# The first stage of the last unit by seven half products

## The chip, the cores and the metric

One core of a Trainium2 chip runs the kernel. The metric is the time of one execution on the device in microseconds. TensorE (PE) multiplies matrices; its weight loads have a row of their own (PEld) and run beside the matmuls. VectorE (DVE) and ScalarE (ACT) read the results from PSUM. GpSimd (POOL) reads SBUF only and issues the loads, and SyncE (SP) issues stores and bounces through HBM.

## The reference

Pooled attention, then a mixer, for 8 batches of 576 rows and 512 columns (8 heads of 64):

```python
k_p = k.reshape(B, H, Sp, pool, D).mean(axis=3)      # pool = 8, so 72 keys
v_p = v.reshape(B, H, Sp, pool, D).mean(axis=3)
attn = softmax(scale * q @ k_p.T)                    # 576 x 72 for each head
x = (attn @ v_p)                                     # as 576 x 512
h = np.maximum(x.T @ w_tok1, 0.0) @ w_tok2           # 576 -> 256 -> 576
u = x + h.T
h2 = np.maximum(u @ w_ch1, 0.0) @ w_ch2              # 512 -> 1536 -> 512
out = u + h2
```

All inputs are fp32; the kernel multiplies in bf16 and adds up in fp32.

## The kernel before

The last two products, `u @ w_ch1` and the one with `w_ch2`, are most of the work. They are done in nine units of 512 rows. Units 0 to 7 take the first 512 rows of batches 0 to 7; unit 8 takes the 8 x 64 rows that are left over, gathered in `uT_tails`.

A unit (`unit_fast`) has two stages. The first makes GT, the maximum with zero of `u @ w_ch1`, transposed: twelve tiles of 128 columns of w_ch1 (`l1_tile`), each of four matmuls 512 columns wide into one PSUM bank, and one evacuation by ScalarE. The second stage multiplies GT by w_ch2 in the way of Strassen and Winograd: seven products of half-sized blocks (`product`, 12 matmuls of 256 columns each) in place of eight. Their operands are sums of blocks of GT, `=3`, `=1`, `=2` and `=4` (`g_sums`, each one VectorE addition of 1536 elements into `area`), and sums of blocks of w_ch2, w0 to w3, made once. In the order of TensorE the products of unit 8 are x, y, z, x again, z again, x again, x again; the other units have an eighth, w. VectorE evacuates them and adds the residual (`plus`); `lo` and `hi` are the two halves of 256 rows of a unit.

A unit is a generator that yields after each half tile (steps 0 to 23) and after each four matmuls of the second stage (24 to 44). `unit` puts other work at the yields, as PLAN says by unit and step: `5.kpT` is the step kpT of batch 5. The names are these.

- `lq`, `lk`, `lv`: the load of a batch's q, k or v, issued by GpSimd's queue and cast to bf16; two buffers each.
- `K0 K1 V0 V1`: pooling of k and v by GpSimd, about 4.3 us each; `kpT`: the pooled keys transposed (TensorE, copied by ScalarE).
- `Q0 Q1`: transposes of q by VectorE (line 284); `s0` to `s2`: scores and exponentials; `av0` to `av4`: times v, divided on VectorE.
- `at0 at1`, `u0` to `u4`: the token products; u ends with a VectorE addition (line 416) into u.
- `M0 M2 M4 M MT`: u out to HBM and back, turned; `T0` to `T5`: its transposes by VectorE into uT (`T4` and `T5` into uT_tails).
- `g`: a gate, one element set by VectorE and copied by GpSimd: what follows in GpSimd's queue waits until VectorE has come so far in its own.

Every engine works through its instructions in the order in which the program lists them. There are four single PSUM banks, p1a to p1d: `take` gives out the one longest given back, and `give` returns a bank as soon as its evacuation is in the program, so a matmul waits on the chip if the bank's last reader isn't done. Scores, av and unit 8's two x tiles use a pair of larger buffers (`p`).

## Time and profile before

| | us |
|---|---|
| median of 3 runs (lowest to highest) | 265.48 (265.43 to 265.86) |
| profiled execution | 264.03 |
| its span, first to last instruction | 262.2 |
| unit 8: first matmul | 239.02 |
| unit 8: second stage begins | 249.38 |
| unit 8: last addition ends | 259.20 |

Times in the text are from the start of the span. A row of the timeline has the start, the length, the engine, the line, the operation, what it writes and reads, the shape and how many, and in brackets how long the engine had been idle and what ended that. A row of the windows has the busy time and the number of instructions of each engine in one stretch.

### The profile page before, as it was taken

The numbers are of one execution on the slowest core, as the hardware profiler recorded it, in microseconds if no ns is written. First come the engines' busy times: TensorE is split into PE (matmuls) and PEld (weight loads), VectorE is DVE, ScalarE is ACT, GpSimd is POOL, SyncE is SP. The second block draws the span as 40 slices with busy tenths as digits, with TensorE's granted clock in tenths as the row PEclk, the third lists the DMA queues.
The fourth block names the chain that finished last, engine by engine and source line by source line (L and its number), as shares of the span: only waits on it lengthen the run. The fifth ranks groups of instructions, "written<-read, shape, count | busy, mean of one in ns | idle before, by whom it ended". The sixth has DMA issues, their size and how long they took to land.

```text
span 262.2 us, 5324 instructions
## 1 busy us (share of the span) xinstructions
PE 255.8 (98%) x2121; PEld 160.4 (61%) x2121; DVE 179.7 (69%) x370; ACT 119.2 (45%) x195; POOL 150.0 (57%) x177
## 2 busy tenths in 40 slices
PE   8899999999999999999999999999999999999994
PEld 3775556754658545864487448744774486486483
DVE  4566489998786657993899449964795486175183
ACT  2445754149465554435641584155535502612610
POOL 8576145999989999999939881988000000101000
PEclk9999999999999999999999999999999999999999
DMA  7999999992096839699357840831414054503204
GB/s 150 191 200 205 206 206 208 207 223 77 2 172 101 133 118 201 146 196 261 66 154 125 239 133 2 162 92 41 123 35 127 5 158 113 129 0 88 75 0 160
DMA packets 31704, 34.29 MB, mean 131 GB/s; under 512 B 3136, under 2 KB 23744, under 8 KB 31680
## 3 DMA queue, kind: packets, MB, share of 16 engines
q0 software_dynamic: 17632, 17.64, 42.6%
q1 hardware_dynamic: 13632, 15.93, 20.4%
q10 hardware_dynamic: 416, 0.39, 0.5%
q8 instruction: 16, 0.26, 0.4%
q14 instruction: 8, 0.07, 0.1%
HBM read 38.99 MB, written 12.58 MB: 197 GB/s over the span
## 4 chain that ended last, share of the span: by engine, by line
PE 80%; POOL 8%; DMA 7%; DVE 3%; issue 1%; POOLq 0%
PE p1d L517 9%; PE p1c L517 9%; PE p1a L517 8%; PE p1b L517 7%; PE p1b L583 7%; PE p1c L583 7%; PE p1a L583 6%; DMA qb<-in_q_dram 5%; PE p1d L583 4%; PE p L297 3%; PE p L379 3%; POOL t L174 2%; POOL t L175 2%; DMA kr<-in_k_dram 2%; PE p L583 2%; PE p1d L393 2%
## 5 line engine op out<-in xcount | busy, mean ns | idle before, releaser
L717 POOL COPY flag<-flag 1x1 f32<-1x1 f32 x47 | 12.6, 269 | 94.5 <-DVE flag L716 94.5
L517 PEld LDWEIGHTS <-w_ch 128*128 128x128 bf16 x432 | 39.6, 98 | 43.4 <-issue 1.8
L583 PEld LDWEIGHTS <-area 128*128 128x128 bf16 x432 | 40.9, 98 | 7.4 <-issue 1.2
L306 ACT ACTIVATE ex<-p 72x768 bf16<-72x768 f32 x42 | 31.6, 803 | 15.9 <-PE p L297 15.7
L583 PEld LDWEIGHTS <-GT 128*128 128x128 bf16 x324 | 30.8, 98 | 8.2 <-issue 2.4
L175 POOL TENSOR_TENSOR t<-t 72x512 f32<-72x512 f32 x23 | 31.0, 1346 | 1.8
L521 ACT ACTIVATE GT<-p1d 128x512 bf16<-128x512 f32 x29 | 17.3, 597 | 27.0 <-PE p1d L517 21.4
L517 PE MATMUL p1d<-uT,w_ch 128*128 128x512 bf16 x104 | 28.8, 379 | 0.0
L174 POOL TENSOR_TENSOR t<-kr 72x1024 f32<-72x1024 bf16 x12 | 25.9, 2155 | 0.5
L517 PE MATMUL p1c<-uT,w_ch 128*128 128x512 bf16 x96 | 26.1, 379 | 0.0
L521 ACT ACTIVATE GT<-p1b 128x512 bf16<-128x512 f32 x26 | 15.6, 598 | 23.2 <-PE p1b L517 16.8
L517 PE MATMUL p1a<-uT,w_ch 128*128 128x512 bf16 x92 | 25.3, 379 | 0.0
L517 PE MATMUL p1b<-uT,w_ch 128*128 128x512 bf16 x92 | 24.2, 379 | 0.0
L174 POOL TENSOR_TENSOR t<-vr 72x1024 f32<-72x1024 bf16 x11 | 24.1, 2187 | 0.3
L521 ACT ACTIVATE GT<-p1a 128x512 bf16<-128x512 f32 x26 | 15.5, 596 | 11.8 <-PE p1a L517 9.2
L521 ACT ACTIVATE GT<-p1c 128x512 bf16<-128x512 f32 x27 | 16.1, 598 | 8.7 <-PE p1c L517 8.3
L384 DVE TENSOR_TENSOR x<-p,den 128x512 bf16<-128x512 f32 x28 | 19.4, 692 | 1.0
L557 DVE TENSOR_TENSOR area<-GT 128x1536 bf16<-128x1536 bf16 x9 | 9.8, 1086 | 12.4 <-ACT GT L521 12.4
L545 DVE TENSOR_TENSOR area<-GT 128x1536 bf16<-128x1536 bf16 x9 | 10.6, 1178 | 10.1 <-ACT GT L521 7.7
L379 PEld LDWEIGHTS <-ex 72*128 72x128 bf16 x280 | 13.4, 98 | 5.6 <-DVE flag L716 0.4
L583 PE MATMUL p1c<-area,area 128*128 128x256 bf16 x120 | 15.4, 273 | 0.0
L379 PE MATMUL p<-vp,ex 72*128 72x65 bf16 x280 | 14.6, 194 | 0.0
(188 smaller groups left out, 461.1 us busy)
## 6 DMA issues: line engine op xcount, KB each, us to landing
out_dram<-o SPq DMA_DIRECT2D x32, 256.0 KB, 4.0
qb<-in_q_dram POOLq DMA_DIRECT2D x7, 576.0 KB, 9.3
kr<-in_k_dram POOLq DMA_DIRECT2D x7, 512.0 KB, 7.4
vr<-in_v_dram POOLq DMA_DIRECT2D x7, 512.0 KB, 9.8
w_ch<-in_moe_w_ch_dram POOLq DMA_DIRECT2D x5, 512.0 KB, 15.8
mem<-u SPq DMA_DIRECT2D x10, 256.0 KB, 2.0
...
```

Of the source, the lines that this page charges most:

```text
L174: eng.tensor_tensor(out=t4[:, 0:n], in0=t[:, hs, 0:4], in1=t[:, hs, 4:8], op=ALU.add)
L175: eng.tensor_tensor(out=t4[:, 0:n, 0:2], in0=t4[:, 0:n, 0:2], in1=t4[:, 0:n, 2:4], op=ALU.add)
L297: nc.tensor.matmul(out=pss[l // 2][0:SP, l % 2, o:o + n1 - n0], lhsT=st["kD"][quad, g, db, :], rhs=st["qD"][quad, g, n0:n1, db], start=(db ...
L306: nc.scalar.activation(out=dst, in_=src, func=AF.Exp, scale=scale)
L379: nc.tensor.matmul(out=ps[:, h // 4, (h % 4) * (D + 1):(h % 4 + 1) * (D + 1)], lhsT=st["ex"][:, h * S + n0:h * S + n0 + P], rhs=st["vp"][: ...
L384: nc.vector.tensor_tensor(out=dst.rearrange("p (a h d) -> p a h d", a=2, d=D), in0=view[:, :, :, 0:D], in1=den[rows, :, :, None].broadcast ...
L517: nc.tensor.matmul(out=ps, lhsT=w_ch1[:, kk, m * P:(m + 1) * P], rhs=uT[kk], start=(kk == 0), stop=(kk == 3))
L521: nc.scalar.activation(out=GT[:, m, :], in_=ps, func=AF.Relu)
L545: nc.vector.tensor_tensor(out=out, in0=a, in1=b, op=ALU.subtract)
L557: nc.vector.tensor_tensor(out=S4[:, 0], in0=GT[:, f, hi], in1=GT[:, sec, hi], op=ALU.add)
L583: nc.tensor.matmul(out=ps[i] if split else ps[:, i], lhsT=chunk(u, i, a(m)), rhs=w(m), start=start and m == 0 and (i == 0 or split), stop= ...
L717: nc.gpsimd.tensor_copy(out=flag[:, 1:2], in_=flag[:, 0:1])
```

## The change

In unit 8 the first stage is also done by seven products of half blocks. Unlike in the second stage, a maximum comes after the blocks are added up, so each of the four output blocks must be complete before it enters GT. The columns of w_ch1 are taken in three groups (a, b, c) of two tiles per half; each group has products 1 to 7, each of four matmuls of 256 columns. Products 1, 6, 7 and 4 add up in one bank and 5 and 3 in a `p` buffer, and 2 has a bank to itself. After products 1, 5 and 6 ScalarE copies the partial sum to SBUF in fp32 (`kept`). Products 2, 3 and 7 are evacuated by a VectorE addition of such a copy, followed by a maximum in place on VectorE or ScalarE (`RELU`); product 4 is evacuated by ScalarE as before. `HALVED` is the order, and the first pieces of x and y of the second stage stand in it.

The operands are sums of blocks of w_ch1 (W0 to W3, in units 6 and 7) and of uT_tails (D80 to D83, in unit 7), all on VectorE, into the buffers that held k and v. PLAN is new for all units: most steps move by a few places, the loads and gates among them. HEAD, the start of the kernel, is unchanged.

```diff
 PLAN = [
-    {0: "0.u3 1.Q0 2.lk 1.kpT", 3: "0.u1", 4: "1.s0 g g", 5: "1.Q1", 9: "1.s1 0.u0", 10: "1.vpool1 1.vpool0 g", 11: "1.s2", 12: "=3 0.u2 2.lq", 13: "1.av1", 14: "1.av3", 16: "1.av2", 18: "w0 3.lk", 19: "1.av0 3.lq", 20: "1.av4 w1 g", 23: "1.at1 2.lv", 24: "1.at0 3.lv =1", 25: "=2 =4", 26: "g", 28: "w3", 31: "1.u1 1.u2", 32: "1.t1", 33: "1.t2 w2", 34: "2.K0", 35: "1.u0", 38: "3.Q1 2.K1", 40: "1.u3", 41: "1.t0", 42: "g", 43: "2.Q0 1.t3", 44: "1.u4 2.V0 2.kpT"},
-    {2: "2.s0", 5: "2.Q1", 6: "2.s2", 9: "3.Q0 3.K0", 11: "3.K1", 12: "2.s1", 16: "2.v1", 17: "4.lq 2.av3 g", 18: "2.av2", 19: "2.av4", 22: "2.av1", 23: "2.av0 =1 =3", 24: "=2", 25: "4.lk g", 26: "g =4", 27: "3.kpT 5.lk 2.at0", 28: "g 3.s1 2.at1", 29: "3.V1", 30: "3.s2 2.u2", 32: "2.u3 3.s0", 33: "2.u0", 37: "2.t3", 39: "2.t0", 40: "2.u1 3.V0", 41: "4.Q1 2.t2", 42: "2.t1", 44: "4.lv"},
-    {2: "3.av4", 3: "3.av0 4.K0", 7: "3.av1", 8: "g 4.K1", 10: "3.av2 3.av3", 13: "g 3.at0", 14: "3.at1 g 6.lk", 16: "4.kpT", 17: "=3", 18: "4.Q0 3.u2", 19: "3.u1", 20: "3.u0", 21: "3.M0", 22: "3.u3 4.s2", 23: "3.M2 4.V1 3.u4", 24: "4.V0", 25: "=1", 26: "=2 3.M4", 27: "4.s0 g", 28: "6.lq", 30: "=4 g", 31: "4.s1 5.lv", 34: "3.M g", 35: "4.av2 3.T1", 36: "3.MT", 38: "3.T2", 40: "3.T3 3.T0", 41: "4.av4", 44: "5.lq 3.T5"},
-    {0: "5.K0 5.K1", 1: "4.av1", 4: "g", 6: "6.lv 4.av0", 7: "4.av3 5.Q0", 9: "5.V1 6.Q0", 10: "4.at1 4.at0", 12: "5.kpT", 13: "4.u2", 14: "4.u1", 15: "g", 16: "5.Q1 4.u3", 17: "5.s0", 19: "3.T4 =3", 21: "4.u0", 23: "=1", 25: "5.V0 4.M0", 26: "=2 5.s1", 27: "g", 29: "=4", 30: "5.s2", 31: "g", 33: "5.av2", 35: "5.av0 5.av1 4.M2 4.M", 39: "5.av3", 40: "4.T2 5.av4", 41: "4.T1", 42: "7.lq 4.T3", 43: "5.at0 4.T0", 44: "5.at1"},
...
-    {18: "=3", 23: "=1", 25: "=2", 30: "=4", 43: "g"},
+    {0: "1.Q0 1.kpT 2.lk 0.u1 0.u3", 3: "1.s0 1.Q1 3.lq", 5: "2.lq g", 9: "1.s1", 10: "g 0.u0 1.vpool0 2.lv", 11: "1.vpool1 1.s2 =3 g", 12: "0.u2", 13: "1.av1", 14: "1.av3", 15: "1.av2", 17: "1.av0", 19: "w0 1.av4", 20: "3.lk g", 21: "3.lv", 23: "w1 1.at1 =1", 24: "=2", 26: "=4", 27: "g w3", 28: "1.at0", 30: "1.u2", 31: "1.u1", 33: "1.t2 1.t1", 34: "2.K0 w2", 36: "1.u0", 39: "3.Q1 1.u3", 40: "2.K1", 43: "1.t0 g 2.Q0 1.t3 1.u4", 44: "2.Q1 2.V0 2.kpT"},
+    {2: "2.s0", 6: "2.s2", 9: "3.K0", 10: "3.K1", 12: "3.Q0 2.s1", 13: "2.v1", 17: "2.av3", 18: "2.av2", 19: "2.av4 4.lq", 21: "g", 22: "2.av0", 23: "2.av1 4.lk", 24: "=1", 25: "g =2", 26: "g 5.lk =3", 27: "=4 3.kpT", 28: "g 2.at0 3.s1 2.at1 3.V1", 31: "3.s2 3.V0 2.u0", 32: "2.u3", 33: "2.u1 3.s0", 34: "2.u2", 37: "2.t3", 39: "2.t0", 41: "4.lv 2.t2", 42: "2.t1", 44: "4.Q1"},
+    {2: "3.av4 4.K0", 5: "3.av0", 7: "g 4.K1 3.av2", 9: "3.av1 g", 11: "3.av3", 13: "3.at0", 14: "3.at1 g =3", 16: "4.Q0", 17: "4.kpT 3.u0", 18: "3.u1", 19: "3.u2", 20: "6.lk", 21: "4.V1 3.M0 3.u3", 22: "4.s2 3.M2 3.u4", 24: "4.V0 g", 25: "4.s0 =1", 27: "6.lq 3.M4", 28: "=2", 29: "=4", 30: "g 4.s1 5.lv", 31: "3.M 3.MT", 32: "g 5.lq", 33: "3.T0", 35: "3.T2", 36: "3.T3", 39: "3.T1", 40: "4.av4", 44: "4.av2"},
+    {0: "5.K1 5.K0 4.av1", 4: "3.T5 g", 5: "6.lv", 6: "5.V1 4.av0", 8: "4.av3", 10: "4.at0 5.Q1 5.Q0 4.at1", 12: "g 4.u2", 13: "6.Q0 5.kpT", 15: "4.u1", 16: "4.u3", 17: "3.T4 5.s0", 18: "=3", 21: "4.u0", 22: "5.V0", 23: "5.s1", 25: "=1", 26: "g", 27: "=2", 29: "5.s2 g", 31: "=4", 32: "5.av1", 33: "4.M0 4.M2 5.av2", 36: "5.av3", 38: "7.lq", 39: "5.av0", 40: "4.M 5.av4 4.T3", 41: "4.T2", 42: "4.T0 4.T1", 43: "5.at0", 44: "6.Q1 5.at1"},
...
+    {5: "6.av0", 6: "6.av1", 7: "7.K0", 8: "6.av3 7.K1", 9: "7.kpT", 12: "6.at0", 13: "7.V0", 14: "7.s1 6.at1", 15: "g 7.V1", 17: "6.u0 6.u3", 18: "6.u2", 20: "6.u1", 21: "6.M2 g", 23: "=3 6.M0", 24: "7.s0 =1", 26: "6.M =2", 27: "=4", 30: "g", 31: "7.av1", 32: "6.T0", 37: "6.T1", 38: "6.T2", 39: "7.s2", 40: "6.T3", 41: "g", 44: "7.av2"},
+    {0: "7.av0", 1: "g", 6: "g", 10: "7.av3", 11: "7.av4", 13: "W0 7.at0", 15: "g 7.at1", 16: "W1", 18: "7.u0", 19: "7.u1", 20: "7.u2 g 7.u3", 21: "=3", 22: "7.M0 g", 24: "g =1 =2", 26: "7.M2", 29: "7.M", 30: "g", 32: "=4", 34: "7.u4 g", 35: "7.T0 7.T1", 36: "7.T2", 37: "7.T3", 38: "7.M4", 41: "g W2", 44: "7.MT g 7.T5"},
+    {1: "g W3", 18: "=3", 20: "g", 22: "g", 23: "=1", 24: "=2", 25: "7.T4", 27: "=4", 32: "D80", 33: "g", 34: "D81", 41: "g", 42: "D82", 44: "D83"},
+    {19: "=3", 21: "=1 =2", 24: "=4", 41: "g"},
...
+    HALVED = {B: "a1 a2 a5 b1 b2 a6 a3 b6 c1 b5 a7 b7 c5 c2 c6 b3 a4 c3 c7 b4 x0 c4 x1 x2 y0 y1 y2"}
+    RELU = dict(a2="D", a3="D", a7="A", b2="D", b3="D", b7="A", c2="D", c3="A", c7="D")
...
+    wide = {}
+
+    def first_weight(k):
+        if k == 0:
+            for key in "kv":
+                t = raw.tile([P, H, POOL, D], BF16, name=key + "r").rearrange("p h i d -> p (h i d)")
+                wide[key] = t[:, 0:4 * DC // 2].rearrange("p (s c n) -> p s c n", s=2, c=2)
+                wide[key, "u"] = t[:, 4 * DC // 2:4 * DC // 2 + 1024].rearrange("p (s c n) -> p s c n", s=2, c=2)
+        c1, c2 = slice(0, 2), slice(2, 4)
+        n1, n2 = slice(0, DC // 2), slice(DC // 2, DC)
+        S1, S2, S3, S4 = (wide[key][:, i] for key in "kv" for i in range(2))
+        if k == 0:
+            nc.vector.tensor_tensor(out=S1, in0=w_ch1[:, c1, n2], in1=w_ch1[:, c2, n2], op=ALU.add)
+        elif k == 1:
+            sub(S2, S1, w_ch1[:, c1, n1])
+        elif k == 2:
+            sub(S3, w_ch1[:, c1, n1], w_ch1[:, c1, n2])
+        else:
+            sub(S4, w_ch1[:, c2, n1], S2)
+
+    def row_sums(n, k):
+        uT = batches[n][2]["uT"] if n < B else uT_tails
+        T1, T2, T3, T4 = (wide[key, "u"][:, i] for key in "kv" for i in range(2))
+        c1, c2 = slice(0, 2), slice(2, 4)
+        if k == 0:
+            sub(T1, uT[:, c1, lo], uT[:, c1, hi])
+        elif k == 1:
+            sub(T2, uT[:, c2, lo], T1)
+        elif k == 2:
+            sub(T3, uT[:, c2, lo], uT[:, c1, lo])
+        else:
+            sub(T4, uT[:, c2, hi], T2)
+
+    def first_halved(n, uT, piece):
+        S1, S2, S3, S4 = (wide[key][:, i] for key in "kv" for i in range(2))
+        T1, T2, T3, T4 = (wide[key, "u"][:, i] for key in "kv" for i in range(2))
+        spare = [raw.tile([P, H, POOL, D], BF16, name=key + "r").rearrange("p h i d -> p (h i d)").bitcast(FP32)
+                 .rearrange("p (s m n) -> p s m n", s=4, m=2) for key in "kv"] if n == min(HALVED) else wide["spare"]
+        wide["spare"] = spare
+
+        def group(g):
+            ms, mt = slice(2 * g, 2 * g + 2), slice(NH + 2 * g, NH + 2 * g + 2)
+            t = {}
+
+            def mm(ps, a, col, b, start, stop):
+                for j in range(2):
+                    for c in range(2):
+                        o = col + (2 * g + j) * P
+                        nc.tensor.matmul(out=ps[:, j], lhsT=a[:, c, o:o + P], rhs=b[c], start=start and j == 0 and c == 0,
+                                         stop=stop and c == 1, skip_group_check=True)
+
+            u1, u2 = ([uT[c] for c in cs] for cs in ((0, 1), (2, 3)))
+            half = lambda b, cols: [x[:, cols] for x in b]
+            rows = lambda T: [T[:, c] for c in range(2)]
+            w1, w2 = w_ch1[:, 0:2], w_ch1[:, 2:4]
+            kept = lambda i: spare[i // 2][:, 2 * (g % 2) + i % 2]
+
+            def added(key, mr, cols, ps, other):
+                nc.vector.tensor_tensor(out=GT[:, mr, cols], in0=ps, in1=other, op=ALU.add)
+                if RELU[key] == "A":
+                    nc.scalar.activation(out=GT[:, mr, cols], in_=GT[:, mr, cols], func=AF.Relu)
+                else:
+                    (nc.vector if RELU[key] == "D" else nc.gpsimd).tensor_scalar(
+                        out=GT[:, mr, cols], in0=GT[:, mr, cols], scalar1=0.0, scalar2=None, op0=ALU.max)
+
+            def p1():
+                t["x"] = take([P, 2, 256], FP32)
+                mm(t["x"], w1, 0, half(u1, hi), True, False)
+                nc.scalar.copy(out=kept(0), in_=t["x"])
+
+            def p2():
+                y = take([P, 2, 256], FP32)
+                mm(y, w2, 0, half(u2, hi), True, True)
+                added("abc"[g] + "2", ms, hi, y, kept(0))
+                give(y)
+
+            def p5():
+                t["z"] = ps_two.tile([P, 2, 512], FP32, name="p2")[:, 0].rearrange("p (m n) -> p m n", m=2)
+                mm(t["z"], S1, 0, rows(T1), True, False)
+                nc.scalar.copy(out=kept(1), in_=t["z"])
+
+            def p6():
+                mm(t["x"], S2, 0, rows(T2), False, False)
+                nc.scalar.copy(out=kept(2), in_=t["x"])
+
+            def p3():
+                mm(t["z"], S4, 0, half(u2, lo), False, True)
+                added("abc"[g] + "3", ms, lo, t["z"], kept(2))
+
+            def p7():
+                mm(t["x"], S3, 0, rows(T3), False, False)
+                added("abc"[g] + "7", mt, lo, t["x"], kept(1))
+
+            def p4():
+                mm(t["x"], w2, DC // 2, rows(T4), False, True)
+                nc.scalar.activation(out=GT[:, mt, hi], in_=t["x"], func=AF.Relu)
+                give(t["x"])
+
+            return {1: p1, 2: p2, 3: p3, 4: p4, 5: p5, 6: p6, 7: p7}
+
+        G = [group(g) for g in range(3)]
+        for s in HALVED[n].split():
+            if s[0] in "abc":
+                G["abc".index(s[0])][int(s[1])]()
+            else:
+                piece(s[0], int(s[1]))
+            yield
...
+        evacuate = {"x": lambda e: plus(part(s1), part(two["x"]), residual(0, 0))(e),
+                    "y": lambda e: plus(cols_of(oa, 0), part(two["y"]), part(s1))(e)}
+        two = {}
+
+        def piece(key, k):
+            split = last and key == "x"
+            t = two[key] = two.get(key) or bank(split)
+            o = NH * (key == "y")
+            for i, m in [(k, m) for m in range(4)] if k < 2 else [(i, m) for i in range(2) for m in (4, 5)]:
+                nc.tensor.matmul(out=t[i] if split else t[:, i], lhsT=chunk(u, i, GT[:, o + m, lo]), rhs=w_ch2[:, o + m, lo],
+                                 start=m == 0 and (i == 0 or split), stop=m == NH - 1, skip_group_check=True)
+                if split and m == NH - 1:
+                    evacuate[key](i)
+
+        if n in HALVED:
+            yield from first_halved(n, uT, piece)
+            x, y = two["x"], two["y"]
...
```

More of the change, by code (lines that the diff above doesn't have):

```diff
@@ L121, in load_kv @@
     def load_kv(b, src, key):
-        t = loaded[b, key] = raw.tile([SP, H, POOL, D], BF16, name=key + "r")
+        t = loaded[b, key] = raw.tile([P, H, POOL, D], BF16, name=key + "r")[0:SP]
         kv(t, src, b, 0, H, 0, BP)
@@ L576, in unit_fast @@
         uT = [u["uT"][:, kk, :] for kk in range(4)]
-        for m in range(NM):
-            yield from l1_tile(n, m, uT)
         def product(ps, a, w, start, after, split=False, end=None):
```

22 lines of the change are left out of this document (14 added, 8 removed), and 5 rows, old and new, of the table PLAN.

## The prediction

> **What bounds the kernel now.** The page's share of the span comes first, then the slices, the windows by stage, and the two places at which TensorE is seen to wait.
>
> ```profile
> PE 255.8 (98%) x2121; PEld 160.4 (61%) x2121; DVE 179.7 (69%) x370; ACT 119.2 (45%) x195; POOL 150.0 (57%) x177
> ...
> PE   8899999999999999999999999999999999999994
> POOL 8576145999989999999939881988000000101000
> PEclk9999999999999999999999999999999999999999
> ```
>
> TensorE is busy 98% at full granted clock, so time comes from its work and from the gaps in it. Listing its starts against their usual spacing (0.216 us for 512 columns, 0.109 for 256) leaves, after the head, three waits: 0.30 us near 47 us, 0.30 near 56 and 0.61 near 125. GpSimd has no pause between 46 and 131 us but at gates: its pooling paces the middle.
>
> ```profile
> 194.90:219.50 24.60, 24.60 (x176) 15.25 (x173) 16.68 (x38) 8.25 (x14) 0.87 (x5) 1.00 0.35 97
> 219.50:239.00 19.50, 19.50 (x134) 12.90 (x132) 9.87 (x29) 7.16 (x12) 2.39 (x10) 1.00 0.28 68
> 239.00:249.40 10.40, 10.40 (x51) 4.73 (x50) 2.25 (x3) 6.57 (x11) 0.00 (x0) 1.00 0.37 102
> 249.40:259.20 9.80, 9.34 (x85) 8.09 (x83) 7.74 (x16) 0.60 (x1) 0.17 (x1) 1.00 0.15 54
> ```
>
> The rows are units 6 and 7, and the first and second stage of unit 8: width, then busy time of PE, PEld, DVE, ACT and POOL. In the first stage of unit 8 VectorE works 2.25 us of 10.4: room for additions, and TensorE is the limit there.
>
> The chain of waits from 105 to 127 us, and the timeline there:
>
> ```profile
> 108.88 0.69 POOL qb L128
> ...
> 111.08 12.19 DMA qb<-in_q_dram
> ...
> 123.30 0.87 DVE qD L284 x2
> ...
> 124.66 0.70 DVE u L416
> ...
> 125.40 0.59 PE p1c L415 x2
> ```
> ```profile
> 118.34 0.69 DVE L384 TENSOR_TENSOR x<-p,den 128x512 bf16<-128x512 f32 x1
> 123.30 1.44 DVE L284 STREAM_TRANSPOSE qD<-qb 128x576 uint32<-128x576 uint32 x2 [4.26 <-DMA qb<-in_q_dram]
> 124.66 0.69 DVE L416 TENSOR_TENSOR u<-p1c,x 128x512 bf16<-128x512 f32 x1
> ```
>
> A late load of q (batch 5) holds VectorE for 4.26 us. The addition of `4.u2` queues behind two transposes, its bank p1c stays taken, and `4.u3`, next to get that bank, waits until 125.40.
>
> **First stage of unit 8.** Removed: 48 matmuls of 512 columns, 48 x 0.2158 = 10.36 us. Added: 7 products x 3 groups x 4 = 84 of 256 columns, 84 x 0.1092 = 9.17. Saved on TensorE at most 1.19 us. Weight loads are 98 ns against 109, as in the second stage. What returns is waiting.
>
> ScalarE goes from 12 to 15 evacuations; back to back they are 0.49 us apart (0.597 less an overlap of 0.11), 7.3 us in 9.2: it fits. The in-place maximum on ScalarE has no row; the cast from SBUF (L694, 576 elements) took 0.671, scaled to 512 this is 0.62, bounded by 0.59 and 0.67.
>
> VectorE gets nine additions of PSUM and fp32 (L626, 0.686, 0.61 apart in a queue) and six in-place maxima without a row. Bounds: 0.16 (the fixed part that 0.307 for 288 and 0.457 for 576 elements leave, L246) and 0.69 (512 elements at the fp32 rate, L384). I take 0.42, from L246's 0.457 scaled to 512, the nearest. Addition and maximum depend on each other (about 0.03 between), so a pair takes 1.06 us of queue. VectorE comes free 1.9 us after the unit's start: unit 7's last two additions (1.29) and the last row sum. In queue order a2, b2, a3, a7, b7, c2, b3, c3, c7 there are five pairs ahead of c7's addition (5.30), three single additions (1.82), its own 0.61 and 0.1 of waiting for c2: it ends at 9.73. `c4`, which adds to the bank that it reads, would start at 9.29 and waits 0.49. c4's maximum ends at 11.08; then `=1` (0.96, to 12.07), `=2` (13.04), two halves of x (13.72), `=4` (14.59), z's evacuation (15.26). The second z product would start at 15.02 and waits 0.29. With small waits at c3, c7 and the last x (0.13), the last addition ends 19.9 us after the unit's start; before it was 259.20 - 239.02 = 20.18. **Gain 0.28 us**; by the bounds of the maximum a gain of 0.6 to a loss of 1.1.
>
> The Trainium skill (VectorE: DVE Perf Modes, The perf-mode tier table) has `tensor_scalar` on bf16 in SBUF run at four elements a cycle, 693 ns for 2048; by its fixed part an estimate for 512 is 0.29 us. Then c4 waits 0.23 and the unit gains 0.55. No row here has that form, so the sum keeps 0.42.
>
> **Operand sums.** Four of 1536 elements (W) at 0.95 (L545) and four of 512 (D) at about 0.42 give 5.5 us on VectorE, which idles 7.9 us in unit 6 and 9.6 in unit 7: cost 0. W0 and W1 stand ahead of unit 6's additions, W2 and D82 behind its evacuations. D80 and D81 (0.7) stand ahead of the evacuation for `x3`, with 0.5 us left. Without cover each would cost its own length. `7.T4` now precedes x's evacuation in unit 7: that ends at 233.71 and x's second product starts at 233.78, so 0 to 0.35; I take 0.
>
> **The plan, early.** In unit 0 `3.lq` goes ahead of `2.lq` and all loads ahead of their old places. The queue is full until 59 us (DMA row all nines), so 2.q lands one load (2.9 us) later than its 46.6: before its transposes at 52.9. 0. `2.K0` stays behind a gate that follows the same five VectorE sums; the two waits of 0.30 stay. `7.kpT` moves from step 15 to 9 of unit 5 (172.4 us); its pooling ended at 173.02, but began behind gates at 161.81 and 162.81, and now needs only one, a step earlier: about 171.9. 0, bounded by 0.6.
>
> **The plan, unit 3.** Now `5.Q1` and `5.Q0` come at step 10, `4.u2` at 12 and `4.u1` at 15. Counting banks in the order in which they are given back, u1 gets u2's. It comes one half tile and one u (0.43 each) sooner than u3 did: 124.79 - 0.86 = 123.93. The bank is free 2.13 us after the load lands (two transposes, one addition, as in the rows: 125.40 - 123.27). Landing at 123.27 again, u1 waits 1.47, a loss of 0.86. When does it land? In unit 1 GpSimd waited 0.58 and 0.43 at gates that stood behind `=3`; the new plan puts these sums behind the gates, so the pooling runs about 1.0 us earlier. Its last V of batch 4 ends at 106.9 for 107.95, and `6.lq` starts there, for 108.83 (the gate's copy took 0.99 in between). `5.lv` is still held by a gate whose VectorE part ended at 108.94, and goes at about 109.2 for 109.69. So 6.q is out of the way when 5.v starts, one load of 2.9 us less: 5.q lands near 120.7. Its bank is free at 122.8, before 123.93. **Gain 0.61 us**; bounds +0.61 and -0.86.
>
> **Sum.** 0.28 + 0.61 = 0.89 us. The profiled execution took 264.03 (span 262.2 and 1.8 around it): 263.14. The median of the runs shown is 265.48, 1.45 above it; on that footing **264.6 us**.
>
> **Rivals.**
> - Slower: the load of q lands as before, because stores and pooling, not the gates, set its time. For it: the four stores of unit 2 fall in the same microseconds. Against: 6.q leaves earlier. u1 waits 1.47: +0.86 - 0.28 = +0.58, 266.1. It turns the sum positive from a landing of 122.7 on, and decides at 123.2. Chance 0.13.
> - The maxima on VectorE run at 0.69: its queue then bounds the first stage, c3 and c4 wait 0.8 each, unit 8 loses 1.08; with the 0.61, +0.47: 265.9. Chance 0.10.
> - The maxima on VectorE take 0.29, inside the bounds: a pair is 0.93, c7's addition ends 0.6 us sooner in VectorE's queue, `c4` waits 0.23 and unit 8 gains 0.55: 264.3. (This is the skill's rule above.) Chance 0.18.
> - Part of the gain: the load lands near 122.4 and unit 3 comes out even, only unit 8's 0.28 stays: 265.2. Chance 0.15.
> - A re-planned unit has a new wait that the rows don't show. Before had three, 1.2 us together; one to two microseconds more give 264.9 to 266.6. Chance 0.16.
> - The forecast: chance 0.28, own range 263.7 to 265.0 (unit 8 from +0.6 to -0.1, unit 3 at 0.61, and 0.3 more if the early waits go).
>
> Within 0.2% (0.53 us) is about what a measurement can't tell from no change. Faster: most of the forecast and of the short maxima, and a little of the others, 0.48. Same: the third rival and parts of the second and fourth, 0.27. Slower: 0.25. The range runs from 263.6 to 266.4.
>
> **What would show it.** TensorE: 84 matmuls of 256 columns in about 9.8 us, waits at `c4` and at z's second product of a few tenths each. VectorE: the in-place maxima at 0.3 to 0.42. Unit 3: the transposes of batch 5 start near 121 and no wait ahead of u1; a start at 123 with 1.4 us ahead of u1 is the first rival. Gates in unit 1 without waits of GpSimd. I am wrong if the span's loss lies in units 0 to 7 at places that are quiet now, or if c3, c7 and x0 wait for VectorE.

## Result and profile after

| | before | after |
|---|---|---|
| median of 22 runs each (lowest to highest), us | 264.75 (263.61 to 265.89) | 263.21 (262.54 to 264.49) |
| ratio, 95% interval | | 0.9946 (0.9930 to 0.9962) |
| profiled execution, us (span) | 264.03 (262.2) | 263.51 (261.7) |
| unit 0, first product, us | 24.18 | 24.73 |
| unit 8, first product to last addition, us | 20.18 | 19.56 |

The changed kernel is faster by 0.54%: 1.4 us by the ratio, 1.5 by the medians. The forecast of 264.6 had the direction, but the time lies 0.4 us below its range. The first four lines are of the page of the changed kernel: busy time of each engine, then the 40 slices of the span.

```profile
PE 253.8 (97%) x2133; PEld 163.5 (62%) x2157; DVE 191.5 (73%) x390; ACT 119.6 (46%) x198; POOL 153.1 (58%) x174
...
PE   7899999999999999999999999999999999999994
...
POOL 8567233999999999899969694996100111101000
PEclk9999999999999999999999999999999999999999
```

VectorE's busy time grows by 11.8 us. TensorE's seems to fall by 2.0, but this trace lacks 24 of its 2157 matmul records; two further profiles of the changed kernel, which have them all, show 255.7 and 255.4 us, for 255.8 before. The granted clock is full throughout. GpSimd's row is still full from 46 to 131 us (slices 8 to 20). The windows by stage (unit 6, unit 7, then unit 8 cut after its product `c4` and at its last addition; busy time and count of PE, PEld, DVE, ACT, POOL):

```profile
194.75:219.61 24.86, 24.75 (x181) 15.52 (x181) 19.00 (x45) 8.36 (x14) 2.84 (x8) 1.00 0.32 96
219.61:239.14 19.53, 19.48 (x133) 12.90 (x132) 12.43 (x29) 7.17 (x12) 2.91 (x7) 1.00 0.28 68
239.14:249.10 9.96, 9.88 (x90) 8.59 (x88) 9.12 (x19) 7.55 (x14) 0.00 (x0) 1.00 0.43 107
249.10:258.71 9.61, 9.08 (x82) 7.72 (x79) 8.53 (x17) 0.67 (x2) 0.00 (x0) 1.00 0.16 57
```

VectorE's busy time in unit 7 rises from 9.87 to 12.43 us and the unit keeps its 19.5. In the first stage of unit 8 it rises from 2.25 in 10.4 us to 9.12 in 9.96: an engine that had room is now busy nine tenths of the time. The timeline of VectorE in unit 8 of the changed kernel (start, length, engine, line, operation, shape, idle time before it):

```profile
240.88 0.68 DVE L634 TENSOR_TENSOR GT<-p1d,kr 128x512 bf16<-128x512 f32 x1
241.60 0.29 DVE L638 TENSOR_SCALAR GT<-GT 128x512 bf16<-128x512 bf16 x1
241.81 0.68 DVE L634 TENSOR_TENSOR GT<-p1b,kr 128x512 bf16<-128x512 f32 x1
...
247.33 0.69 DVE L634 TENSOR_TENSOR GT<-p,vr 128x512 bf16<-128x512 f32 x1
247.94 0.68 DVE L634 TENSOR_TENSOR GT<-p1d,kr 128x512 bf16<-128x512 f32 x1
248.65 0.29 DVE L638 TENSOR_SCALAR GT<-GT 128x512 bf16<-128x512 bf16 x1
248.86 0.95 DVE L547 TENSOR_TENSOR area<-GT 128x1536 bf16<-128x1536 bf16 x1
```

The maximum in place, which had no row before, takes 0.29 us, and the next instruction follows 0.21 after its start. c7's addition (247.94) ends at 248.62, and TensorE's product `c4`, which adds to the bank that it reads, starts right behind it:

```profile
247.98 0.60 PE L758 MATMUL p<-w_ch,GT 128*128 128x256 bf16 x4
248.67 0.60 PE L624 MATMUL p1d<-vr,w_ch 128*128 128x256 bf16 x4
```

Four matmuls of 256 columns take 0.44, so `c4` could have started at 248.42: a wait of 0.25. (The bracket of a row counts idle time from the modelled end of the matmul before; the waits of TensorE in this text are, as in the prediction, taken from the spacing of its starts.) z's second product waits 0.23 more, and these two are all that unit 8 waits for.

In unit 3 the load of q5 still lands late, but earlier than before. GpSimd of the changed kernel first, with the gate copies and the issue of the loads, then VectorE:

```profile
105.67 1.33 POOL L182 TENSOR_TENSOR vp<-t 72x256 bf16<-72x256 f32 x1
106.94 0.97 POOL L843 COPY flag<-flag 1x1 f32<-1x1 f32 x1
107.86 0.75 POOL L130 DMA_DIRECT2D qb<-in_q_dram  x1
109.44 0.17 POOL L843 COPY flag<-flag 1x1 f32<-1x1 f32 x1 [0.82 <-DVE flag L842]
109.55 1.26 POOL L120 DMA_DIRECT2D vr<-in_v_dram  x2
110.81 0.17 POOL L843 COPY flag<-flag 1x1 f32<-1x1 f32 x1
110.93 0.72 POOL L130 DMA_DIRECT2D qb<-in_q_dram  x1
```
```profile
106.93 0.94 DVE L547 TENSOR_TENSOR area<-area,GT 128x1536 bf16<-128x1536 bf16 x1
...
119.23 0.69 DVE L386 TENSOR_TENSOR x<-p,den 128x512 bf16<-128x512 f32 x1
122.49 1.44 DVE L286 STREAM_TRANSPOSE qD<-qb 128x576 uint32<-128x576 uint32 x2 [2.56 <-DMA qb<-in_q_dram]
123.86 0.72 DVE L418 TENSOR_TENSOR u<-p1a,x 128x512 bf16<-128x512 f32 x1
```

The first gate copy takes 0.97 us where the next two take 0.17, and it ends 0.04 us behind VectorE's sum in the first line of the second view; the load of q6 (107.86) leaves only then. VectorE now waits 2.56 us for the load of q5 where it waited 4.26, and TensorE's wait at this place falls from 0.61 to 0.09. Yet unit 8 starts at 239.14, for 239.02 before. The table says why: unit 0 itself began 0.55 later, behind HEAD, which the change does not touch. Counted from unit 0, unit 8 starts 214.41 us on, for 214.84. Two profiles, one of each kernel, don't settle the gain of the plan; that is what the experiments had to do.

### The profile page after: what moved, and what is told of

It is laid out like the page before. It is cut to its first block, busy times and chain, and to the rows that moved or that the text cites. A ratio compares the mean times of both kernels' runs of the same rounds, so it can differ in the third digit from the quotient of the medians.

```text
span 261.7 us, 5407 instructions
## 1 busy us (share of the span) xinstructions
PE 253.8 (97%) x2133; PEld 163.5 (62%) x2157; DVE 191.5 (73%) x390; ACT 119.6 (46%) x198; POOL 153.1 (58%) x174
## 5 line engine op out<-in xcount | busy, mean ns | idle before, releaser
L843 POOL COPY flag<-flag 1x1 f32<-1x1 f32 x44 | 17.0, 387 | 79.7 <-DVE flag L842 79.7
L519 PEld LDWEIGHTS <-w_ch 128*128 128x128 bf16 x384 | 34.7, 98 | 38.7 <-issue 2.5
L690 PEld LDWEIGHTS <-GT 128*128 128x128 bf16 x300 | 28.9, 98 | 6.1 <-issue 0.9
L523 ACT ACTIVATE GT<-p1b 128x512 bf16<-128x512 f32 x23 | 13.7, 597 | 23.1 <-PE p1b L519 15.2
L523 ACT ACTIVATE GT<-p1c 128x512 bf16<-128x512 f32 x25 | 15.0, 598 | 17.1 <-PE p1c L519 10.7
L523 ACT ACTIVATE GT<-p1d 128x512 bf16<-128x512 f32 x28 | 16.7, 597 | 11.8 <-PE p1d L519 8.7
L519 PE MATMUL p1a<-uT,w_ch 128*128 128x512 bf16 x78 | 21.1, 379 | 0.1
L418 DVE TENSOR_TENSOR u<-p1a,x 128x512 bf16<-128x512 f32 x12 | 8.7, 723 | 16.1 <-PE p1a L417 10.1
L120 POOL DMA_DIRECT2D kr<-in_k_dram x17 | 10.9, 645 | 9.5 <-DMA w_ch<-in_moe_w_ch_dram 3.4
L523 ACT ACTIVATE GT<-p1a 128x512 bf16<-128x512 f32 x20 | 12.0, 599 | 6.8 <-PE p1a L519 6.2
L559 DVE TENSOR_TENSOR area<-GT 128x1536 bf16<-128x1536 bf16 x9 | 9.8, 1093 | 6.4 <-ACT GT L523 6.3
```

The source lines that it names most:

```text
L120: nc.gpsimd.dma_start(out=t[j0:j1, h0:h1].rearrange("j h i d -> j h (i d)"), in_=src[b, h0:h1].rearrange("h (j i) d -> j h (i d)", i=POOL) ...
L418: nc.vector.tensor_tensor(out=rows_of(c), in0=blocked(ps), in1=blocked(x), op=ALU.add)
L519: nc.tensor.matmul(out=ps, lhsT=w_ch1[:, kk, m * P:(m + 1) * P], rhs=uT[kk], start=(kk == 0), stop=(kk == 3))
L523: nc.scalar.activation(out=GT[:, m, :], in_=ps, func=AF.Relu)
L559: nc.vector.tensor_tensor(out=S4[:, 0], in0=GT[:, f, hi], in1=GT[:, sec, hi], op=ALU.add)
L690: nc.tensor.matmul(out=ps[i] if split else ps[:, i], lhsT=chunk(u, i, a(m)), rhs=w(m), start=start and m == 0 and (i == 0 or split), stop= ...
```

## Experiments

Theory at the start: the last unit gives what the profile shows, 0.61, and the plan the rest, by an earlier load in unit 3. Rivals: the plan gives nothing and the rest is chance; the rest comes from other waits than that of unit 3.

**The two halves.** First the kernel before, with the new plan of units 0 to 7 less the operand sums; unit 8 stays as it was. (One of the eight rows is shown, that of unit 7.)

```diff
 PLAN = [
...
-    {5: "g", 6: "g", 11: "g", 18: "g", 24: "=1", 26: "7.T4 =2 =4", 32: "g", 35: "g =3", 39: "g"},
+    {1: "g", 18: "=3", 20: "g", 22: "g", 23: "=1", 24: "=2", 25: "7.T4", 27: "=4", 33: "g", 41: "g"},
...
 ]
```

> The kernel before with the new plan of units 0 to 7 alone: no sums of w_ch1 and uT_tails, unit 8's first stage and its row of the plan as before. Theory (the gain has two parts, about 0.6 us in unit 8 and the rest, 0.8 of the measured 1.42, in the plan): 0.8 us faster than before, ratio 0.997, unit 8 again 20.2 us from its first matmul to its last addition. Rival (the plan moves the wait in unit 3 and gains nothing, as the two profiles suggest: unit 8 begins at 239.14 against 239.02): ratio 1.000 within 0.001.

Measured: 263.98 us (12 runs) against 264.48 for the kernel before (35 runs), ratio 0.9965 (0.9936 to 0.9993). In the profile u1 waits 0.63 behind the transposes of q5. VectorE first, then TensorE, of this kernel:

```profile
122.52 1.44 DVE L284 STREAM_TRANSPOSE qD<-qb 128x576 uint32<-128x576 uint32 x2 [3.10 <-DMA qb<-in_q_dram]
123.89 0.72 DVE L416 TENSOR_TENSOR u<-p1a,x 128x512 bf16<-128x512 f32 x1
```
```profile
124.66 0.59 PE L415 MATMUL p1a<-AT,w_tok 128*128 128x512 bf16 x2 [0.46 <-DVE u L416]
```

The plan alone is worth something (the interval excludes zero), unit 8 takes 20.18 as expected, and the bank that u1 gets is u2's, as the prediction counted; here unit 3 began 0.5 earlier than in the changed kernel's profile and the load landed at the same time, so u1 waited. This one profile hardly shows the gain: from the first product to unit 8 it takes 214.81 us, for 214.93 on average in seven profiles of the kernel before.

Then the kernel after, with the old plan of units 0 to 7 and in it the operand sums, at the steps that they have in the new one. (Again the row of unit 7.)

```diff
 PLAN = [
...
-    {1: "g W3", 18: "=3", 20: "g", 22: "g", 23: "=1", 24: "=2", 25: "7.T4", 27: "=4", 32: "D80", 33: "g", 34: "D81", 41: "g", 42: "D82", 44: "D83"},
+    {1: "W3", 5: "g", 6: "g", 11: "g", 18: "g", 24: "=1", 26: "7.T4 =2 =4", 32: "g D80", 34: "D81", 35: "g =3", 39: "g", 42: "D82", 44: "D83"},
...
 ]
```

> The old plan of units 0 to 7 with the eight operand sums put in at the steps of the new plan; unit 8 as changed. Theory: the half products alone give 0.6 us, ratio 0.9977, unit 8 19.6 us long, the wait ahead of 4.u3 near 125 us stays (0.6). Rival (all of the measured gain is unit 8's, and the plan is worth nothing): 1.4 us, ratio 0.9946, which the profile would have to show as a unit 8 of 18.8 us.

Measured: 264.52 us, ratio 0.9994 (0.9965 to 1.0024). Unit 8 takes 19.56, but unit 7 takes 20.05 instead of 19.53. VectorE and TensorE in unit 7 of this kernel:

```profile
236.34 0.42 DVE L547 TENSOR_TENSOR kr<-uT_tails 128x512 bf16<-128x512 bf16 x1
...
236.80 0.42 DVE L547 TENSOR_TENSOR kr<-uT_tails,kr 128x512 bf16<-128x512 bf16 x1
237.14 0.75 DVE L733 TENSOR_TENSOR s<-p1d,u 128x256 f32<-128x256 f32 x2
237.81 0.95 DVE L547 TENSOR_TENSOR area<-GT 128x1536 bf16<-128x1536 bf16 x1
```
```profile
238.82 1.48 PE L690 MATMUL p1d<-area,area 128*128 128x256 bf16 x12 [0.34 <-DVE area L547]
```

The old plan has VectorE's sum `=3` at step 35 of unit 7, behind D80, D81 and an evacuation. With 0.84 us of operand sums ahead of it, it ends at 238.76, and x3, which reads it, starts at 238.82: a wait of 0.50. So the operand sums eat most of the 0.61 in the old plan, and the median shows about nothing. Unit 6, where W0 to W2 are made, takes 24.60, as before. The theory's 0.6 for the whole was wrong, the rival's unit 8 of 18.8 too.

**That sum alone.** The kernel after, with `=3` of unit 7 back at step 35.

```diff
-    {1: "g W3", 18: "=3", 20: "g", 22: "g", 23: "=1", 24: "=2", 25: "7.T4", 27: "=4", 32: "D80", 33: "g", 34: "D81", 41: "g", 42: "D82", 44: "D83"},
+    {1: "g W3", 20: "g", 22: "g", 23: "=1", 24: "=2", 25: "7.T4", 27: "=4", 32: "D80", 33: "g", 34: "D81", 35: "=3", 41: "g", 42: "D82", 44: "D83"},
```

> The changed kernel with one item moved back: VectorE's sum =3 of unit 7 from step 18 to step 35, behind the operand sums D80 and D81, where the old plan has it. Theory (the operand sums cost nothing only because =3 was moved out of their way): TensorE waits about 0.5 us ahead of the product x3 of unit 7, near 238 us, unit 7 takes 20.0 instead of 19.5 and the whole is about 0.5 us longer than the changed kernel. Rival (that wait came from something else of the old plan): unit 7 stays at 19.5 to 19.6.

```profile
237.05 1.48 PE L690 MATMUL p1b<-area,area 128*128 128x256 bf16 x12 [0.31 <-DVE area L547]
```

TensorE waits 0.48 ahead of x3 and unit 7 takes 20.02 (218.35 to 238.37): the theory holds. The whole, 262.77, is not longer than the changed kernel's profiled executions, since unit 0 began at 23.82 in this one. From there it takes 238.95, 0.30 more than the changed kernel on average (table below); the 0.5 expected of the whole can't be read from one execution.

**The order around u1.** In unit 3 of the kernel before (first two lines), `5.Q0` goes behind the two u's; in that of the kernel after, `5.Q0` and `5.Q1` go behind u1.

```diff
-    {0: "5.K0 5.K1", 1: "4.av1", 4: "g", 6: "6.lv 4.av0", 7: "4.av3 5.Q0", 9: "5.V1 6.Q0", 10: "4.at1 4.at0", 12: "5.kpT", 13: "4.u2", 14: "4.u1", 15: "g", 16: "5.Q1 4.u3", 17: "5.s0", 19: "3.T4 =3", 21: "4.u0", 23: "=1", 25: "5.V0 4.M0", 26: "=2 5.s1", 27: "g", 29: "=4", 30: "5.s2", 31: "g", 33: "5.av2", 35: "5.av0 5.av1 4.M2 4.M", 39: "5.av3", 40: "4.T2 5.av4", 41: "4.T1", 42: "7.lq 4.T3", 43: "5.at0 4.T0", 44: "5.at1"},
+    {0: "5.K0 5.K1", 1: "4.av1", 4: "g", 6: "6.lv 4.av0", 7: "4.av3", 9: "5.V1 6.Q0", 10: "4.at1 4.at0", 12: "5.kpT", 13: "4.u2", 14: "4.u1 5.Q0", 15: "g", 16: "5.Q1 4.u3", 17: "5.s0", 19: "3.T4 =3", 21: "4.u0", 23: "=1", 25: "5.V0 4.M0", 26: "=2 5.s1", 27: "g", 29: "=4", 30: "5.s2", 31: "g", 33: "5.av2", 35: "5.av0 5.av1 4.M2 4.M", 39: "5.av3", 40: "4.T2 5.av4", 41: "4.T1", 42: "7.lq 4.T3", 43: "5.at0 4.T0", 44: "5.at1"},
...
-    {0: "5.K1 5.K0 4.av1", 4: "3.T5 g", 5: "6.lv", 6: "5.V1 4.av0", 8: "4.av3", 10: "4.at0 5.Q1 5.Q0 4.at1", 12: "g 4.u2", 13: "6.Q0 5.kpT", 15: "4.u1", 16: "4.u3", 17: "3.T4 5.s0", 18: "=3", 21: "4.u0", 22: "5.V0", 23: "5.s1", 25: "=1", 26: "g", 27: "=2", 29: "5.s2 g", 31: "=4", 32: "5.av1", 33: "4.M0 4.M2 5.av2", 36: "5.av3", 38: "7.lq", 39: "5.av0", 40: "4.M 5.av4 4.T3", 41: "4.T2", 42: "4.T0 4.T1", 43: "5.at0", 44: "6.Q1 5.at1"},
+    {0: "5.K1 5.K0 4.av1", 4: "3.T5 g", 5: "6.lv", 6: "5.V1 4.av0", 8: "4.av3", 10: "4.at0 4.at1", 12: "g 4.u2", 13: "6.Q0 5.kpT", 15: "4.u1 5.Q0", 16: "4.u3 5.Q1", 17: "3.T4 5.s0", 18: "=3", 21: "4.u0", 22: "5.V0", 23: "5.s1", 25: "=1", 26: "g", 27: "=2", 29: "5.s2 g", 31: "=4", 32: "5.av1", 33: "4.M0 4.M2 5.av2", 36: "5.av3", 38: "7.lq", 39: "5.av0", 40: "4.M 5.av4 4.T3", 41: "4.T2", 42: "4.T0 4.T1", 43: "5.at0", 44: "6.Q1 5.at1"},
```

> The kernel before with one step moved: the transpose 5.Q0 of unit 3 goes from step 7 to step 14, behind the additions of 4.u2 and 4.u1, so that a late load of q no longer holds them. Theory: the wait of 0.61 ahead of 4.u3 goes, the scores at step 17 wait little (the load lands at 123.3, the transpose is done by 124.8), 0.5 to 0.7 us faster, ratio 0.9975. Rival (the load holds the scores instead, or GpSimd's pooling takes the time back later): ratio 1.000.

> The changed kernel with the same edit: 5.Q0 goes from step 10 of unit 3 to step 15 behind 4.u1, 5.Q1 to step 16. If the load still sets the time of 4.u1 in most executions (in the profile it landed at 122.4 and u1 waited 0.09 with a late head): 0.3 to 0.6 us faster than the changed kernel, ratio to before 0.9925 to 0.993. If the plan has removed the wait: the same as the changed kernel, 0.9946.

The first gave 264.37, ratio 0.9995 (0.9966 to 1.0024). Its wait ahead of u3 is gone and unit 3 takes 29.62, for 30.24 in the first profile and 30.04 on average in seven, as meant, but the profiled execution has 0.72 for the load of v1 near 31 us and 0.44 near 47 in its place; the interval holds both zero and the 0.6 us expected. The second gave 263.49, ratio 0.9955 (0.9932 to 0.9978), like the changed kernel. u1 waits no more, and the scores of batch 5 wait 0.35 instead:

```profile
126.79 0.53 PE L299 MATMUL p<-qD,kD 32*72 32x384 bf16 x8 [0.18 <-DVE qD L286]
```

In the changed kernel the place of the transposes is worth nothing that these intervals show; one wait is exchanged for another, and both end with the load of q5.

**The price of the maximum, and who does it.** Three variants of the new last unit. The first issues each of VectorE's six maxima twice:

```diff
+                    for _ in range(2):
                         (nc.vector if RELU[key] == "D" else nc.gpsimd).tensor_scalar(
```

> The changed kernel with each of VectorE's six maxima in the last unit issued twice; the second repeats the first on the same place, so the values are the same. Theory (the price of VectorE's maximum is what sets how much the new first stage gains): VectorE is busy without a gap from c2's addition on, each further maximum takes 0.21 of its time, c4 then waits about 0.7 us instead of 0.25, and unit 8 takes 20.1 to 20.4 us instead of 19.56, from its first product to its last addition: about the gain of 0.28 that was forecast with a maximum of 0.42, or nothing at all. Rival (the products set the length, the maxima are hidden): unit 8 stays at 19.6.

```profile
241.13 0.62 DVE L639 TENSOR_SCALAR GT<-GT 128x512 bf16<-128x512 bf16 x2
...
248.49 0.68 DVE L634 TENSOR_TENSOR GT<-p1d,kr 128x512 bf16<-128x512 f32 x1
249.21 0.63 DVE L639 TENSOR_SCALAR GT<-GT 128x512 bf16<-128x512 bf16 x2
```

Unit 8 takes 20.71, above the 20.1 to 20.4 expected: a second maximum on the same place, which has to wait for the first, costs 0.33 and not 0.21. Six of them, 2.0 us on VectorE, cost the unit 1.15: `c4` waits 0.78 and z's second product 0.35, and c3, which adds to the bank that c5's copy reads, waits 0.55 for that copy. In proportion, the 0.13 by which the prediction overpriced each maximum costs about 0.45 (an estimate), which would leave a gain of 0.16. So the price of this one instruction sets how much the stage gains, and the rival falls: with the maxima doubled the gain of 0.61 is a loss of 0.53.

The second puts all nine maxima on ScalarE:

```diff
-    RELU = dict(a2="D", a3="D", a7="A", b2="D", b3="D", b7="A", c2="D", c3="A", c7="D")
+    RELU = dict(a2="A", a3="A", a7="A", b2="A", b3="A", b7="A", c2="A", c3="A", c7="A")
```

> The changed kernel with all nine maxima of the last unit on ScalarE. Theory (each engine's share is what it can take): nine maxima of 0.62, nine copies at 0.49 a piece and three of c4's kind at 0.61 are 11.8 us on ScalarE, where there are 10.1 from the first copy to the last result; the copies come late, the additions that read them wait, and unit 8 takes 20.8 to 21.5 us, longer than the 20.18 before the change. Rival (VectorE alone sets the end): its six maxima taken off shorten unit 8 by 0.4 to 19.1 to 19.3.

Unit 8 takes 23.46, 3.9 more than in the changed kernel, far beyond both expectations. The copies do come late and the additions wait, but not because ScalarE's time runs out. The window of its first stage, ScalarE, and TensorE there:

```profile
238.47:251.30 12.83, 9.88 (x85) 8.04 (x83) 7.42 (x12) 9.21 (x18) 0.00 (x0) 1.00 0.34 83
```
```profile
240.93 0.63 ACT L636 ACTIVATE GT<-GT 128x512 bf16<-128x512 bf16 x1 [1.19 <-DVE GT L634]
241.47 0.57 ACT L655 COPY kr<-p 128x512 f32<-128x512 f32 x1
```
```profile
242.09 0.60 PE L624 MATMUL p<-uT_tails,vr 128*128 128x256 bf16 x4 [0.83 <-ACT kr L655]
```

ScalarE is busy 9.21 of 12.83 us: it isn't full. It stands idle 1.19 us at the first maximum, which waits for VectorE's addition, and the copy of product 5 that is queued behind it lets TensorE wait 0.83 (0.99 by the starts). Addition, maximum, copy and product form a ring over three engines. By the starts TensorE waits 4.4 us in this unit (0.99, 0.55, 1.43, 0.22, 0.57 and 0.07 in the first stage, 0.56 at z's second product), for 0.48 in the changed kernel: that is the 3.9. The changed kernel gives ScalarE only maxima whose addition ends shortly before.

The third moves one maximum, c2's, to ScalarE at a place where ScalarE has room, behind the result of a4:

```diff
-    RELU = dict(a2="D", a3="D", a7="A", b2="D", b3="D", b7="A", c2="D", c3="A", c7="D")
+    RELU = dict(a2="D", a3="D", a7="A", b2="D", b3="D", b7="A", c2="L", c3="A", c7="D")
...
+                if RELU[key] == "L":
+                    later.append(GT[:, mr, cols])
...
+                while later:
+                    v = later.pop()
+                    nc.scalar.activation(out=v, in_=v, func=AF.Relu)
```

> The changed kernel with one maximum, c2's, moved from VectorE to ScalarE, where it stands behind the result of a4. Theory (VectorE's row of additions and maxima from c2 on to the last addition has no gap, so that 0.21 less on it shortens the unit by as much): c4 waits 0.05 instead of 0.25, and unit 8 takes 19.3 to 19.4 us instead of 19.56; too little to see in the median of the whole kernel. Rival (the wait ahead of c4 is replaced by one for ScalarE): 19.5 to 19.6.

Measured: unit 8 19.56, unchanged; the kernel 263.28 (12 runs), ratio 0.9961 (0.9936 to 0.9986).

```profile
245.17 0.69 DVE L635 TENSOR_TENSOR GT<-p,vr 128x512 bf16<-128x512 f32 x1 [0.18 <-PE p L625]
245.90 0.29 DVE L641 TENSOR_SCALAR GT<-GT 128x512 bf16<-128x512 bf16 x1
246.17 0.69 DVE L635 TENSOR_TENSOR GT<-p,vr 128x512 bf16<-128x512 f32 x1
```

The theory fell. VectorE now waits 0.18 for b3's product, and c3's addition starts 8.18 us after the unit (246.17 less 237.99), where it started 8.19 after it before (247.33 less 239.14). VectorE's row had no gap, but it had no backlog either: each addition came just as its product was ready. What a saved maximum frees there is at once spent waiting. A dearer maximum, as the doubled one shows, does make a backlog.

**Where the plan's gain lies.** Copies of both kernels were profiled again, six of the kernel before and two of the kernel after; the second copy of the kernel after was also timed.

> The kernel before, unchanged, profiled once more, to see where its executions differ. Theory A (the plan's gain lies in waits for loads that only some executions have): its executions differ by 0.5 us or more, and the difference stands in TensorE's waits for the loads of v1 (near 31 us), of q5 (ahead of u1, near 124 us) and for copies behind GpSimd, so that a longer execution has a longer sum of such waits. Theory B (the plan's gain is a fixed wait that every execution had): the waits are those of the first profile, 0.30 near 47, 0.30 near 56 and 0.61 near 124.6, and unit 8 starts within 0.2 us of 239.0.

> As for the copy above: theory A, other waits for loads than in the first profile and a start of unit 8 that moves with their sum; theory B, the same three waits. Both expect 20.17 us for unit 8, from its first product to its last addition.

> The changed kernel, unchanged, profiled once more. Theory A: no single wait above 0.3 us from unit 1 on, whatever the first unit's start, and unit 8 starts before 239.2. Theory B: the same as in its first profile (waits of 0.25, 0.16 and 0.15). Both expect 19.56 for unit 8.

> The changed kernel, unchanged, timed and profiled once more beside the kernel before. Theory A (the plan also takes away waits for loads that only part of the old kernel's executions have): its median is 1.2 to 1.6 us below the kernel before, and its times lie closer together (half of them within 0.9 us, against 1.0 to 1.3 before). Theory B (the change takes away fixed waits only): 1.0 to 1.1 us below, with the same spread. Both expect 19.56 for unit 8.

> The kernel before, unchanged, profiled again to catch an execution above 264.6 us. Theory A (waits of the old plan): from the first product of unit 0 to the end the execution takes longer than the 239.7 us of the others, by waits above 0.3 us in units 0 to 3 that the others do not have. Theory B (the start): from the first product of unit 0 on it takes 239.6 to 239.9, and its length lies in a first product after 25.0 us.

> As for the copy above: theory A, over 240.0 us from the first product of unit 0 to the end in an execution above 264.6; theory B, 239.6 to 239.9 and a late first product.

> As for the two copies above: theory A, over 240.0 us from the first product of unit 0 to the end in an execution above 264.6; theory B, 239.6 to 239.9 and a late first product.

> As for the three copies above: theory A, over 240.0 us from the first product of unit 0 to the end in an execution above 264.6; theory B, 239.6 to 239.9 and a late first product.

The timed copy took 263.11 (10 runs) against 264.62, ratio 0.9941 (0.9919 to 0.9962): the gain repeats. In the table, "time" is that of the profiled execution, "start" the first product of unit 0, "from there" their difference; then the waits of TensorE at five places, near 31, 47 (in the kernel after two, at 47 and 52), 56, 125 and 143 us. All in us; a dash is less than 0.1.

| execution | time | start | from there | v1 | 47 | 56 | q5 | 143 |
|---|---|---|---|---|---|---|---|---|
| before, first | 264.03 | 24.18 | 239.85 | - | 0.30 | 0.30 | 0.61 | - |
| before, copy 1 | 263.47 | 23.81 | 239.66 | - | 0.30 | 0.30 | 0.44 | - |
| before, copy 2 | 264.50 | 24.84 | 239.66 | - | 0.30 | 0.30 | 0.43 | - |
| before, copy 3 | 264.62 | 24.03 | 240.59 | 0.73 | 0.41 | 0.29 | 0.52 | - |
| before, copy 4 | 263.87 | 24.37 | 239.50 | 0.16 | 0.30 | 0.29 | 0.14 | - |
| before, copy 5 | 264.80 | 24.77 | 240.03 | - | 0.69 | 0.29 | 0.34 | - |
| before, copy 6 | 264.29 | 24.11 | 240.18 | 0.45 | 0.44 | 0.29 | 0.38 | - |
| after, first | 263.51 | 24.73 | 238.78 | 0.25 | 0.24 | 0.16 | - | 0.15 |
| after, copy 1 | 263.46 | 24.79 | 238.67 | - | 0.24 | 0.15 | 0.10 | 0.16 |
| after, copy 2 | 262.98 | 24.47 | 238.51 | - | 0.24 | 0.15 | - | 0.16 |

TensorE in copy 3 of the kernel before, at three of these places:

```profile
32.09 0.71 PE L264 MATMUL p1c<-vr,ident 72*72 72x256 bf16 x5 [0.57 <-DMA vr<-in_v_dram]
...
48.25 0.59 PE L415 MATMUL p1d<-AT,w_tok 128*128 128x512 bf16 x2 [0.24 <-DVE o L626]
...
126.01 0.38 PE L415 MATMUL p1c<-AT,w_tok 128*128 128x512 bf16 x1 [0.36 <-DVE u L416]
```

And VectorE and TensorE in copy 2 of the kernel after, at the last of them:

```profile
121.92 1.44 DVE L286 STREAM_TRANSPOSE qD<-qb 128x576 uint32<-128x576 uint32 x2 [2.51 <-DMA qb<-in_q_dram]
```
```profile
124.08 0.59 PE L417 MATMUL p1a<-AT,w_tok 128*128 128x512 bf16 x2
124.51 0.59 PE L519 MATMUL p1c<-uT,w_ch 128*128 128x512 bf16 x2
```

From the first product on, the kernel before takes 239.92 us on average and the kernel after 238.65: 1.27 less. From the first product of a unit to that of the next, unit 0 is 0.33 shorter, unit 2 0.06 and unit 3 0.28; unit 5 is 0.27 shorter and unit 6 0.26 longer, as `7.av0` moved from the one to the other. That is 0.68 before unit 8. Unit 8 is 0.61 shorter, and behind its last addition the kernel after takes 0.03 more. The variants agree: over eight profiles with each plan (those of the table, the one of the old plan with the operand sums, and five variants with the new plan) units 0 to 6 take 195.51 and 194.82 us, 0.69 less.

Most of the 0.68 is in the waits: those at q5 fall from 0.41 on average to under 0.1, those near 47 from 0.39 to 0.24, those near 56 from 0.29 to 0.15, and a new one of 0.16 comes near 143. These places make 0.48. The load of v1 is waited for in some executions of both kernels; it is issued in the head, which is the same, so that its average (0.19 before, 0.08 after) is put down to chance, which no run tests. The last 0.09 lie in steps below 0.1.

Of the two theories on the longer executions, the waits (A) hold for copy 3, whose start is early and whose 240.59 are the longest. Copy 5 has both a late start (24.77) and a wait of 0.69. The late start alone (B) is refuted in that no execution started after 25.0. In the first two copies neither theory named what makes their difference: they are 1.03 us apart, all of it in the start. Theory B, fixed waits, holds in them near 47 and 56, not at q5 (0.44 and 0.43 for 0.61), and falls near 47 with copies 3, 5 and 6. The first copy of the kernel after kept to theory A (no wait above 0.3, unit 8 at 238.99). The timed copy has the median that theory A gave it, 1.5 below, but hardly a smaller spread than the kernel before: the middle half of its times lies within 0.7 us, against 0.85. Still open is the difference between 1.27 in the profiles and 1.5 in the medians; it is within the intervals (1.0 to 1.9 us for the first ratio), and none of the profiles of the kernel before is of an execution above 265 us.

## Why the prediction was wrong

The direction was right, and so were the queue of unit 8 and the count of banks in unit 3. What put the time below the range is the footing. The terms of the gain were off in both directions, and their sum was too small.

**The footing.** "The median of the runs shown is 265.48, 1.45 above it": the step that failed. Over 22 runs the same kernel has a median of 264.75, and in later sets 264.48 and 264.62. The three times shown were from the upper half of a spread of 2.3 us. The range of 263.6 to 266.4 was laid from 265.48; from 264.75 the same range would be 262.9 to 265.7 and hold the measured 263.21. As a difference, too, it held the result: it went down to a gain of 1.9 us, and 1.5 were measured. On the profiled execution's own footing the forecast was 263.14, and the changed kernel's three profiled executions took 262.98 to 263.51.

**First stage of unit 8: predicted 0.28, measured 0.61.** The mis-sized term is the maximum on VectorE, "I take 0.42", measured 0.29. It was scaled from L246, a copy of 576 elements out of a PSUM bank; the maximum reads and writes SBUF. At 0.29 the prediction's own queue gave a wait of 0.23 at `c4` and a gain of 0.55; measured are 0.25 and 0.61. So the count of the queue was right and its price was wrong. The predicted 0.62 of a maximum on ScalarE is measured at 0.63, the additions' 0.686 at 0.68, and z's second product waits 0.23 for 0.29 predicted.

The Trainium skill (VectorE: DVE Perf Modes, The perf-mode tier table) has this form run at four elements a cycle, and the estimate from its 693 ns for 2048 elements was 0.29. The trace agrees: 0.29.

**Operand sums: predicted 0, measured 0.** Unit 7 takes 19.53 in both kernels. But the reason given, "0.5 us left" ahead of x3, left out that the old plan has `=3` in the same queue. The cover is the move of `=3` from step 35 to 18; without it the sums cost 0.48 to 0.50. The prediction weighed neither that move nor what was late without it.

**The plan, early: predicted 0, measured 0.33 in unit 0.** Here "the two waits of 0.30 stay" failed. They were tied to a gate, and the gate is indeed still there. In all 18 profiles unit 1 begins 9.6 us after GpSimd starts to pool k of batch 2, behind that gate, so the gate sets the end of unit 0. In the shortest executions the pooling starts 22.73 us after unit 0 in the old plan and 22.62 in the new one, and unit 0 takes 32.33 and 32.20: a fixed gain of 0.13. The rest is in delays that only some executions have: six of nine with the old plan are more than 0.1 us longer, by up to 0.84, and three of nine with the new one, by up to 0.42. Whether the plan or chance lessens these wasn't separated by a run, nor which of the moved steps brings the gate forward. `7.kpT` has no wait, as predicted.

**The plan, unit 3: predicted 0.61, measured 0.28.** The bank count was right: in the kernel with the plan alone u1 waits for u2's bank. The landing, "near 120.7", was wrong by a size: counted from the start of unit 0 it was 96.5, and measured are 97.8, 97.5 and 97.5 (transposes at 122.49, 122.29 and 121.92), for 99.1 before. All that follows counts from there too. The pooling came even earlier than predicted (V of batch 4 ends at 82.0 to 82.3, for 82.7), but the gate's copy again took 0.97, and `6.lq` left at 82.9 to 83.1 instead of 82.7. The term that failed is "one load of 2.9 us less". `6.lq` leaves 1.7 us ahead of `5.lv`, for 0.86 before and 2.3 counted, and from issue to landing q5 takes 11.5 us, for 11.7 to 12.2 in the kernel before: about 0.5 less. An advance of 1.3 to 1.6 instead of 2.6 is just enough: the wait is 0.1 or none, and 0.63 and 0.41 where the load came late (the plan alone; all maxima on ScalarE). The rest of the 0.61 was the kernel before's: its wait there is 0.14 to 0.61, 0.41 on average, and the one profile at hand had the longest. The new wait of 0.16 near 143 us, at the end of this unit, takes part of it back.

**The rivals.** The short maximum came true. The load did not land as before, so the first rival fell. "Part of the gain", with a load that "lands near 122.4", gave the landing of the first profile (122.5), but unit 3 doesn't come out even there (29.76 for 30.24): the landing moves with the start of the execution, and so does u1. A new wait came, at 143 us, but of 0.16 and not of one to two us. Two figures there don't follow from their terms: one to two microseconds more than 264.6 are 265.6 to 266.6, not 264.9 to 266.6, and the forecast's own range, with 0.6, 0.61 and 0.3 off 265.48, begins at 264.0, not 263.7.

| term | predicted | measured |
|---|---|---|
| unit 8 | 0.28 | 0.61 |
| early plan (unit 0) | 0 | 0.33 |
| unit 3, with the new wait at 143 us | 0.61 | 0.28 |
| all else | 0 | 0.05 |
| sum | 0.89 | 1.27 (medians 1.5) |
